# Gated linear attention with a soft mixture of experts: scores by halves with a lasting zero quarter, F32R parts of the log magnitudes, hats in one product, more warming products

## The chip, the cores and the metric

The kernel runs on one core of a Trainium2 chip. The metric is the device time of one execution in microseconds. The core has five engines that matter here, each working through its own list of instructions in order: TensorE (PE in the profile; its weight loads are PEld), VectorE (DVE), ScalarE (ACT), GpSimd (POOL) and SyncE (SP), which here issues the DMA transfers. They wait for each other by semaphores. [...]

## The reference, cut to what matters

Attention has 4 batches, 8 heads, 768 tokens and 48 channels a head. A complex state of 48 x 48 per head decays per channel by a complex gate and takes in the outer product of k and v:

```
mag = sqrt(a_re**2 + a_im**2); scale = minimum(mag, 0.999) / (mag + 1e-6)
for t in range(S):
    S_re, S_im = ar*S_re - ai*S_im + kv[t], ar*S_im + ai*S_re     # a scaled
    y[t] = q[t] @ S_re
```

The outputs, 3072 tokens of 384 channels, go through a soft mixture of 8 experts with 4 slots each: logits = x @ phi; a softmax over all tokens makes 32 slot inputs, each expert is relu(s @ w1) @ w2 with 1024 hidden units, and a softmax over the slots mixes the expert outputs back for every token.

## The kernel before, in words

The recurrence is turned into matrix products over blocks of 128 tokens; a block g is one of 24 (4 batches of 6), three blocks make a unit u, 8 units in all. Tokens of a block lie on the 128 partitions, in an order that `_order` gives: it differs for even and odd blocks (parity), so that the first and last token of a block come to lie where neighbours need them.

For each unit, `gates` (ScalarE and VectorE by turns, L636-658) turns the gates' real parts into log magnitudes and the imaginary parts into tangents, in place in the tile `aat`; `arctan` makes the angles. Then for each block:

- `phase` (L667-691): a triangle of ones (`tri_u`) times the angles sums them over the block (`up`, L676), VectorE removes whole turns (`n` by adding and taking off a magic number, L679; `f = up - n`, L681), and ScalarE takes sine and cosine into `cs`. For blocks that continue a batch, one row takes over the last phase (L673).
- `expo` (L698-711): a triangle (`tri_l`) times the log magnitudes (`lp`, L702, an F32 product of 384 columns), two exponentials into `ee`, and a small transfer of the last row to DRAM (`rows`) for the state's decay.
- `mults` (L719-737): `ee` times q and k (L723; L728 for the first block), then the two hats (`hat0` of q, `hat1` of k), each `ee` times `cs`, on VectorE (L732, two instructions of 768 elements).
- `xpose` (L741-747): transposes of hats on TensorE (`tp`, L744), copied to `hT` by ScalarE.
- `score` (L749-756): four heads at a time, keys times queries, four products of 128 weight columns by 128 columns (`sp`, L752), then one VectorE product with the causal mask `C_MK` over 128 x 512 (`scT`, L756), two buffers.
- `attend` (L764-782): values times scores (L777), state times queries (L779), into `yb`, two heads by turns at PSUM rows 0 and 64, 48 rows each; copied by ScalarE.
- `delta` (L784-797): keys times values (`db`, L790), added to the state `st` and decayed.
- `xform` (L799): output back to tokens-by-channels (`xp`, L802).

The mixture's logits (`lg`, L109), shares and slot sums (`sip`, L173) run per unit between the blocks. At the end come merging, the experts' hidden products (`hp`, L229), the second layer (`op`, L259), and the outputs (`o`, L288, L298; products of F32R operands), with stores by SyncE. The weights of the experts are loaded in 23 chunks (`wload`, L622) into buffers as they come free: 7 `wx` buffers, then those of gates and q/k, then room of closed pools.

The order of all this is written out by hand in the string `ORDER`. Each name (`x17` is the 17th transpose task, `g3` the gates of group 3) stands once for each step of a task; `run` takes the steps in this order and pins every engine's instructions to it. So the string sets what each engine does next; `g` groups, weight loads (`w`), loads of units (`la`, `lq`, `lv`), the first loads (`i`), activation tables (`L`, `T`) and warming products (`wu`) are placed there too. A warming product (`warm`, L901) is an F32 product of 512 columns whose result is not used; before there are four, of the constants.

Of the kernel before, what the change touches and what calls it, by code (L numbers as in the profile page):

```python
# [86 lines left out]
class _Moe:  # L87
# [223 lines left out]
    i0 L0 g0 g0 g0 i6 i1 wu2 wu1 g0 g0 g0 g0 i3 g0 g0 i4 i2 g1 g1 e0 i8 g1 g1 la0 i7 e0 e0 wu0 lv0 T0 t0 g1 t1 e0 p0 p0 p0 p0 p0  # L311
    L1 m0 m0 m0 p1 g1 g1 x0 x0 i5 x2 p1 g1 g1 m0 m0 x2 p1 p2 g2 g2 g2 g2 lq0 e1 e1 e1 x3 x3 e2 e2 e1 e2 x1 x1 p2 g2 g2 D0 e2 D0
    p2 T1 p1 p1 p1 m1 p2 p2 p2 c0 t2 c0 a0 L2 g2 c1 m1 g2 x6 x6 m1 x7 p3 x5 x5 x7 p3 m2 c1 x4 a0 g2 e3 c3 m2 x8 x10 m2 x4 c2 la1
    g3 g3 g3 p3 c3 e3 e3 x11 d0 e5 e5 p4 D0 e5 g3 x10 a0 x8 D1 e4 e4 c2 D1 e3 g3 D1 p4 p4 e4 f0 D1 g3 g3 x9 a1 f0 a1 x9 c4 x11
    wu3 c5 g3 T2 p3 p3 p3 e4 a1 m4 p5 p5 m3 c4 la2 c5 D2 D2 a2 t3 m3 x14 x14 p4 m3 p5 p4 p4 p6 g3 p5 p5 x12 x12 a2 a2 p5 e5 g4
    D2 D3 D3 m4 m4 x16 x16 x15 x15 p6 D2 p6 x18 m5 p7 x13 x13 l0 p7 L3 x18 m5 m5 l0 p7 D3 g4 g4 f1 f1 x17 p8 x17 c6 e7 e7 e7 f2
    g4 c6 c7 f2 e6 e6 e6 x23 x23 x19 g4 g4 lq1 p8 e8 a3 c7 a3 l0 s0 e8 p8 g4 d1 q0 q0 e8 x20 w0 x19 x20 g4 D3 a3 T3 p6 p6 p8 c8
    c8 p8 g4 x21 x21 c9 c9 D4 D4 D4 x22 e6 x22 m6 p7 p7 a4 a4 D4 c10 c11 lv1 m6 x26 t4 p7 p9 m6 p9 c10 p8 p9 a4 x25 x24 s0 D5 D5
    e7 m7 e8 L4 a5 c11 a5 x25 x24 c12 x26 p10 m7 la3 g5 x28 m7 q0 s0 q0 p10 f3 c12 x27 a5 g5 d2 D5 a6 q0 g5 x28 D6 f3 p10 q0 g5
    x30 x30 x27 m8 g5 m8 x29 e9 e9 m8 e9 x31 x31 e10 e10 e9 l1 l1 e10 g5 c13 c13 x29 x34 x34 e11 c14 e11 lq2 e11 g5 p11 g5 c14  # L320
    q1 f4 f4 q1 q1 T4 D6 D6 x33 x35 x35 x32 x32 g5 p11 a6 a6 p11 p11 p9 p9 p9 c15 c15 s0 s0 s0 x33 p11 e10 m10 a7 a7 p10 c17 m9
    p10 t5 c16 a7 p11 D6 lv2 D7 D7 m9 x36 p10 q1 q1 p12 c16 la4 a8 c17 a8 g6 L5 e11 g6 g6 x38 x38 q1 e13 m9 p12 a8 x39 x39 lv3
    e12 D7 D8 D8 x36 e12 e12 x37 m10 x42 p13 m10 x37 g6 w1 l1 s1 x40 c18 x40 g6 x42 c19 D7 g6 x43 x41 e13 e13 d3 c18 a9 c19 a9
    a9 x41 m11 D8 D9 x43 m11 m11 e12 e14 e14 e14 g6 g6 f7 p13 p13 p14 x47 x47 lq3 m12 f7 T5 c21 c21 p12 c20 D9 p12 c20 p12 x45
    t6 x46 x46 x45 s1 p14 D8 f5 f5 x44 p14 x44 a10 a10 s1 l2 la5 p15 p15 m12 x50 D9 x50 e13 m12 p13 p13 p13 c22 e14 g6 x49 x48
    x49 x48 p14 p14 c22 p14 D10 D10 a10 l2 q2 c23 p15 D9 d4 p15 p16 p16 g7 p15 p15 q2 c23 x51 x51 m13 m13 f6 s1 f6 a11 a11 a11
# [756 lines left out]
```

## Time and profile before

| | |
|---|---|
| median of 3 runs | 300.86 us (299.57 to 302.11) |
| the profiled execution | 302.44 us, span 300.6 us |
| busy time TensorE, VectorE, ScalarE | 271.5, 236.5, 213.5 us |
| mean granted clock of TensorE | 0.960 |
| DMA | 54.85 MB, of it 49.61 MB read from HBM |

The span runs from the first to the last instruction. Busy time is the union of an engine's instructions; two that overlap count once. A matmul of F32 leaves two records in the profile, one of F32R leaves one; their ends are modelled, so distances from start to start are more telling than lengths. In a group's row stand line, engine, operation, tiles, shapes and count, then the busy time and the mean length of one in ns, and last the idle time ahead with what ended it. The granted clock is the share of full speed that TensorE's throttle let through.

### The profile page before, as it was taken

The page shows a single profiled execution, that of the slowest core. Times are in us where ns is not written, and L with a number is a line of the kernel's source. Part 1 is how long each engine was busy: PE and PEld are TensorE (multiplying, and loading weights), DVE is VectorE, ACT ScalarE, POOL GpSimd, SP SyncE. Part 2 cuts the span into 40 slices and gives each one's busy share as a digit, 9 for nine tenths or more (in the row PEclk, how much of TensorE's full clock was granted, in tenths as well). Part 3 has the DMA queues.
Part 4 walks back from the last instruction along what each step waited for, and adds up shares of the span by engine and source line. Part 5 has one row for each costly group of instructions (what it writes and reads, how often), then busy time and mean ns, then how long its engine had stood idle before and what let it go on. Part 6 is the DMA issues. An engine that isn't in the chain of part 4 may idle for free.

```text
span 300.6 us, 6641 instructions
## 1 busy us (share of the span) xinstructions
PE 271.5 (90%) x2694; PEld 214.2 (71%) x2694; DVE 236.5 (79%) x453; ACT 213.5 (71%) x377; POOL 2.8 (1%) x7
## 2 busy tenths in 40 slices
PE   0649599989999999899999999999999999999990
PEld 0135488778888877888878887888898997336760
DVE  1468789899999999999998999998979565714350
ACT  4878979789997997896998797996737444402240
POOL 0000000000000000000000000000000002100000
PEclk9966779989999999999999999999999999999997
DMA  6980720391730493735027990456816496589495
GB/s 244 422 219 3 75 86 3 98 313 48 142 98 2 80 295 89 186 126 160 3 15 302 354 375 11 14 190 240 218 19 266 148 423 256 241 342 423 184 384 200
DMA packets 20788, 54.85 MB, mean 182 GB/s; under 512 B 11536, under 2 KB 13456, under 8 KB 16144
## 3 DMA queue, kind: packets, MB, share of 16 engines
q1 hardware_dynamic: 20752, 54.37, 55.2%
q8 instruction: 23, 0.38, 0.6%
q14 instruction: 13, 0.11, 0.1%
HBM read 49.61 MB, written 4.76 MB: 181 GB/s over the span
## 4 chain that ended last, share of the span: by engine, by line
PE 65%; DMA 12%; ACT 11%; DVE 7%; issue 2%; SPq 0%; DVEq 0%; ACTq 0%
PE sp L752 12%; PE tp L744 11%; DMA aat<-in_aa_dram 8%; PE yb L777 6%; PE db L790 5%; DMA rows<-ee 5%; PE lp L702 4%; PE yb L779 4%; PE up L676 4%; PE hp L229 3%; PE op L259 3%; PE xp L802 3%; PE lg L109 2%; PE ep L277 2%; ACT gt L642 2%
## 5 line engine op out<-in xcount | busy, mean ns | idle before, releaser
L747 ACT COPY hT<-tp 96x512 f32<-96x512 f32 x96 | 53.5, 583 | 17.9 <-PE tp L744 17.8
L744 PE MATMUL tp<-cst,hat 128*96 128x128 f32 x384 | 57.2, 287 | 4.0 <-DVE hat L732 3.8
L744 PEld LDWEIGHTS tp<-cst,hat 128*96 128x96 f32 x384 | 45.0, 134 | 13.5 <-issue 5.8
L752 PE MATMUL sp<-hT,hT 96*128 96x128 f32 x384 | 51.6, 282 | 0.9 <-ACT hT L747 0.9
L752 PEld LDWEIGHTS sp<-hT,hT 96*128 96x128 f32 x384 | 47.2, 194 | 5.3 <-issue 2.5
L732 DVE TENSOR_TENSOR hat<-ee,cs 128x768 f32<-128x768 f32 x48 | 44.6, 951 | 2.3 <-PE tp L744 0.9
L777 PE MATMUL yb<-scT,vt 128*48 128x128 f32 x384 | 37.2, 280 | 3.5 <-DVE scT L756 3.5
L756 DVE TENSOR_TENSOR scT<-sp,cst 128x512 f32<-128x512 f32 x48 | 32.6, 684 | 3.7 <-PE sp L752 3.5
L790 PEld LDWEIGHTS db<-vt,hat 128*96 128x96 f32 x320 | 30.2, 165 | 4.2 <-issue 1.7
L790 PE MATMUL db<-vt,hat 128*96 128x48 f32 x320 | 30.8, 246 | 1.3 <-DVE st L795 1.3
L779 PE MATMUL yb<-hT,st 96*48 96x128 f32 x320 | 31.2, 272 | 0.0
L777 PEld LDWEIGHTS yb<-scT,vt 128*48 128x48 f32 x384 | 21.2, 123 | 11.2 <-issue 3.9
L723 DVE TENSOR_TENSOR ee<-ee,qkt 128x768 f32<-128x768 f32 x23 | 21.8, 951 | 4.8 <-DMA rows<-ee 3.3
L676 PE MATMUL up<-aat,cst 128*128 128x384 f32 x48 | 21.5, 532 | 3.2 <-ACT aat L665 2.9
L702 PE MATMUL lp<-aat,cst 128*128 128x384 f32 x48 | 21.5, 531 | 0.9 <-DVE aat L658 0.5
L779 PEld LDWEIGHTS yb<-hT,st 96*48 96x48 f32 x320 | 19.2, 123 | 0.0
L782 ACT COPY yT<-yb 128x512 f32<-128x512 f32 x24 | 14.0, 582 | 6.5 <-PE yb L779 6.5
L648 DVE TENSOR_TENSOR aat<-aat,gt 128x1152 f32<-128x1152 f32 (+2 forms) x9 | 11.0, 1219 | 8.8 <-ACT gt L646 8.8
L805 ACT COPY xs<-xp 128x384 f32<-128x384 f32 x24 | 11.3, 476 | 8.6 <-PE xp L802 8.6
L679 DVE TENSOR_SCALAR n<-up 128x384 f32<-128x384 f32 x24 | 13.2, 550 | 2.6 <-PE up L676 2.5
L802 PE MATMUL xp<-cst,yT 128*128 128x128 f32 x96 | 14.4, 274 | 0.4 <-DVE scT L756 0.4
L706 ACT ACTIVATE ee<-lp 128x384 f32<-128x384 f32 x24 | 11.8, 492 | 4.2 <-PE lp L702 4.0
(134 smaller groups left out, 418.6 us busy)
## 6 DMA issues: line engine op xcount, KB each, us to landing
aat<-in_aa_dram SPq DMA_DIRECT2D x7, 1152.0 KB
qkt<-in_qk_dram SPq DMA_DIRECT2D x7, 1152.0 KB
wx<-in_w_dram SPq DMA_DIRECT2D x7, 1024.0 KB
wx<-in_w_dram SPq DMA_DIRECT2D x5, 1152.0 KB
vt<-in_vv_dram SPq DMA_DIRECT2D x8, 576.0 KB
out_dram<-os SPq DMA_DIRECT2D x8, 384.0 KB
we<-in_w_dram SPq DMA_DIRECT2D x2, 1152.0 KB
wt<-in_w_dram SPq DMA_DIRECT2D x2, 1152.0 KB
```

The source lines that it names most:

```text
L676: PE.matmul(out=up, lhsT=tri_u[par], rhs=ph, start=True, stop=True)
L702: PE.matmul(out=lp, lhsT=tri_l[par], rhs=aat[u][:, 0, j], start=True, stop=True)
L723: DVE.tensor_tensor(out=e, in0=e, in1=qkt[u][:, j], op=ALU.mult)
L732: DVE.tensor_tensor(out=x, in0=e[:, w].rearrange("p (h d) -> p h d", d=D).unsqueeze(2).broadcast_to([P, H, 2, D]), in1=cs[g], op=ALU.mult,)
L744: PE.transpose(out=tp[:, a, :], in_=hat[g][w][:, 4 * hh + a].rearrange("p c d -> p (c d)"), identity=ident)
L747: ACT.copy(out=hT[g, hh, w], in_=tp)
L752: PE.matmul(out=sp[:, a, :], lhsT=hT[g, hh, 1][:, a, :], rhs=hT[g, hh, 0][:, a, :], start=True, stop=True)
L756: DVE.tensor_tensor(out=t, in0=sp, in1=mask[g % 2].unsqueeze(1).broadcast_to([P, 4, P]), op=ALU.mult)
L777: PE.matmul(out=o, lhsT=vt[u][:, j, h, :], rhs=scT[g, hh][:, a, :], start=True, stop=first)
L779: PE.matmul(out=o, lhsT=st[g - 1][:, h, :], rhs=hT[g, hh, 0][:, a, :], start=False, stop=True)
L790: PE.matmul(out=db[:, h, :], lhsT=hat[g][1][:, h].rearrange("p c d -> p (c d)"), rhs=vt[u][:, j, h, :], start=True, stop=True)
L802: PE.transpose(out=xp[:, c].rearrange("p a d -> p (a d)"), in_=yT[g][:, c, :], identity=ident)
```

## The change

- **Scores by halves.** In a block's order the two halves of 64 partitions are early and late tokens (odd blocks have them swapped). A score of four heads becomes eight products: for each head, the early keys (64 weight columns) with all 128 queries, and the late keys with the late 64 queries. Late keys with early queries, all masked to zero, are not computed: that quarter of each of four lasting tiles (`masked`) is set to zero once by GpSimd. Odd heads have the rows of the halves swapped, so that a pair of heads writes the two halves of PSUM's rows; for them the values are loaded a second time with swapped halves (`vs`, `vst`). VectorE's one mask product becomes three: late queries for all rows (256 elements), and early queries for the 64 early rows of even and of odd heads (128 elements each, 64 partitions).
- **F32R parts.** The log magnitudes are split into an F32R part `hi` (a copy by ScalarE) and the rest `lo` (a subtraction by VectorE), as two more steps of `gates`; `lp` becomes two F32R products that add up. The triangle is copied to an F32R tile once (`tr0`).
- **Phase.** The magic number is added by ScalarE (`n`), VectorE takes it off and subtracts `up` in one instruction; the sign of `f` turns and the sines' scales with it.
- **Hats in one product.** One VectorE instruction of 1536 elements per block for both hats, two buffers of the pair.
- **Warming.** Fourteen warming products in place of four, of a zero tile `blank`, so that they need no transfer; they stand in `ORDER` among the first steps, the last two further behind.
- **Buffers and loads.** 6 `wx` buffers in place of 7; the last weight chunk is loaded into a room of its own at the pools' swap; output tiles take other buffers; the scratch memory for dynamic DMA is set to 1024. The first loads come in another order: all gates of unit 0, the constants, phi, v, the masks, the gates of unit 1, and only then q and k.
- **ORDER** is another string throughout.

The core of the diff:

```diff
+HB = P // 2
+FIRST = (0, HB)
+LAST = (HB, 0)
 def _order(parity):
-    o = list(range(P))
-    for p, t in SWAPS[parity]:
-        o[p] = t
+    o = [(p + HB * parity) % P for p in range(P)]
+    a, b = LAST[parity], LAST[parity] + HB - 1
+    o[a], o[b] = o[b], o[a]
...
 def gates(x):
...
         DVE.scalar_tensor_tensor(out=ar, in0=ar, scalar=W_MAX, in1=t, op0=ALU.min, op1=ALU.subtract)
+        yield "g9"
+        hi, lo = (w[:, j0:j1] for w in parts[u])
+        ACT.activation(out=hi, in_=ar, func=AF.Copy)
+        yield "g10"
+        DVE.tensor_tensor(out=lo, in0=ar, in1=hi.bitcast(F32), op=ALU.subtract)
...
 def phase(u, j):
...
-        DVE.tensor_scalar(out=n, in0=up, scalar1=MAGIC, scalar2=MAGIC, op0=ALU.add, op1=ALU.subtract)
+        ACT.activation(out=n, in_=up, func=AF.Identity, bias=kb[:, 4:5])
+        yield "p2b"
-        DVE.tensor_tensor(out=f, in0=up, in1=n, op=ALU.subtract)
+        DVE.scalar_tensor_tensor(out=f, in0=n, scalar=MAGIC, in1=up, op0=ALU.subtract, op1=ALU.subtract)
...
 def expo(u, j):
...
-        PE.matmul(out=lp, lhsT=tri_l[par], rhs=aat[u][:, 0, j], start=True, stop=True)
+        for x in range(2):
+            PE.matmul(out=lp, lhsT=tri_r[par], rhs=parts[u][x][:, j], start=x == 0, stop=x == 1)
...
 def mults(g):
...
+        DVE.tensor_tensor(out=e, in0=e, in1=qkt[u][:, j], op=ALU.mult)
+        yield "m0"
+        x = wk.tile([P, 2, H, 2, D], F32, name="hat", bufs=BUF["hat"])
+        DVE.tensor_tensor(
+            out=x,
+            in0=e.rearrange("p w (h d) -> p w h d", d=D).unsqueeze(3).broadcast_to(sh),
+            in1=cs[g].unsqueeze(1).broadcast_to(sh),
+            op=ALU.mult,
+        )
...
 def score(g, hh):
+        lo = HB * par
+        early, late_ = slice(lo, lo + HB), slice(HB - lo, P - lo)
-        for a in range(4):
-            PE.matmul(out=sp[:, a, :], lhsT=hT[g, hh, 1][:, a, :], rhs=hT[g, hh, 0][:, a, :], start=True, stop=True)
+        for c in range(2):
+            for rows_, cols in ((early, slice(0, P)), (late_, late_)):
+                for b in range(2):
+                    a = 2 * c + b
+                    o = (rows_.start + HB * b) % P
+                    PE.matmul(out=sp[o : o + HB, a, cols], lhsT=hT[g, hh, 1][:, a, rows_], rhs=hT[g, hh, 0][:, a, cols], start=True, stop=True)
         yield "c1"
-        DVE.tensor_tensor(out=t, in0=sp, in1=mask[g % 2].unsqueeze(1).broadcast_to([P, 4, P]), op=ALU.mult)
+        t = masked[par][hh % BUF["scT"]]
+        DVE.tensor_tensor(
+            out=t[:, :, :, late_], in0=sv[:, :, :, late_], in1=mask[par][:, :, late_].unsqueeze(1).broadcast_to([P, 2, 2, HB]), op=ALU.mult
+        )
+        for b in range(2):
+            o = (lo + HB * b) % P
+            r = slice(o, o + HB)
+            DVE.tensor_tensor(
+                out=t[r, :, b, early], in0=sv[r, :, b, early], in1=mask[par][r, b, early].unsqueeze(1).broadcast_to([HB, 2, HB]), op=ALU.mult
+            )
...
 def attend(g):
...
-                            PE.matmul(out=o, lhsT=vt[u][:, j, h, :], rhs=scT[g, hh][:, a, :], start=True, stop=first)
+                            w = vst[u][:, j, h // 2, :] if b else vt[u][:, j, h, :]
+                            PE.matmul(out=o, lhsT=w, rhs=scT[g, hh][:, a, :], start=True, stop=first)
...
 def warm(x):
-        PE.matmul(out=wp, lhsT=ident, rhs=cst[:, 0:512], start=True, stop=True)
+        PE.matmul(out=wp.rearrange("p (a c) -> p a c", a=4), lhsT=blank, rhs=blank.unsqueeze(1).broadcast_to([P, 4, P]), start=True, stop=True)
...
-    for x in range(4):
+    for x in range(14):
         at("wu", warm, x)
```

More of the change, by code (lines that the diff above doesn't have):

```diff
@@ L310 @@
 ORDER = """
[L311 to L326, printed above, removed]
@@ new lines @@
+    p6 a2 e4 m4 c5 p6 la2 p5 p5 x15 f1 g3 e5 x12 f1 x12 p6 D2 a2 g3 D3 a2 D3 m5 g4 x14 x14 L3 x13 x13 p7 p7 p7 w0 wu9 m4 g4 c7
+    g3 m5 l0 l0 x18 x18 p7 g4 c7 q0 q0 f0 f0 f2 f2 l0 s0 e6 e6 x19 x19 e6 g4 c6 e7 e7 lv1 x17 x17 g4 g4 d1 e7 p8 x16 x16 c9 e8
+    e8 e8 c6 D2 e6 e7 g4 q0 g4 D3 T3 m6 p8 a3 p8 t4 c9 c8 x22 x21 x20 la3 c8 x23 x22 q0 a3 a3 p6 e8 p8 d2 D4 D4 p6 p6 D3 a4 x21
+    a4 p8 g4 s0 p8 p8 p9 x20 c10 p9 lq2 p7 p7 p7 m6 x23 c11 D4 D5 c10 x25 g4 x26 m7 p9 D4 L4 p9 s0 s0 p10 a4 q0 x27 m7 g5 g5 q0
@@ L561, in _polar @@
     tri_u = [cst[:, C_TU : C_TU + P], cst[:, C_TU + P : C_TL]]
-    tri_l = [cst[:, C_TL : C_TL + P], cst[:, C_TL + P : C_MK]]
-    mask = [cst[:, C_MK : C_MK + P], cst[:, C_MK + P : C_SEL]]
+    tri_t = cp.tile([P, 2 * P], F32R, name="tri_t")
+    tri_r = [tri_t[:, 0:P], tri_t[:, P : 2 * P]]
+    mask = [cst[:, C_MK + 2 * P * x : C_MK + 2 * P * (x + 1)].rearrange("p (b t) -> p b t", b=2) for x in range(2)]
     ones = cst[:, C_ONE:C_END]
-    kb = cp.tile([P, 4], F32, name="kb")
+    kb = cp.tile([P, 5], F32, name="kb")
     DVE.memset(kb[:, 0:1], 1.0)
@@ L582, in _polar @@
     moe = _Moe(nc, cp, ys, ps2, cst, phi_sb)
-    aat, qkt, vt = {}, {}, {}
+    aat, qkt, vt, vst = {}, {}, {}, {}
     def load_a(u):
@@ L596, in load_v @@
         SP.dma_start(out=vt[u], in_=vv[u])
+        vst[u] = io.tile([P, UB, 4, D], F32, name="vst")
+        SP.dma_start(out=vst[u], in_=vs[u])
     def load_first(x):
-        if x == 0:
+        if x in (0, 3, 4) and 0 not in aat:
             aat[0] = io.tile([P, 2, UB, HD], F32, name="aat")
-        if x == 2:
+        if x in (2, 7) and 0 not in qkt:
             qkt[0] = io.tile([P, UB, 2, HD], F32, name="qkt")
@@ L658, in gates @@
         DVE.scalar_tensor_tensor(out=ar, in0=ar, scalar=W_MAX, in1=t, op0=ALU.min, op1=ALU.subtract)
+        yield "g9"
+        if u not in parts:
+            parts[u] = [eo.tile([P, UB, HD], F32R, name=f"w{x}", bufs=1) for x in range(2)]
+        hi, lo = (w[:, j0:j1] for w in parts[u])
+        ACT.activation(out=hi, in_=ar, func=AF.Copy)
+        yield "g10"
+        DVE.tensor_tensor(out=lo, in0=ar, in1=hi.bitcast(F32), op=ALU.subtract)
     cs, fr = {}, {}
@@ L910, in _polar @@
         at("i", load_first, x)
+    at("tr", lambda: DVE.tensor_copy(out=tri_t, in_=cst[:, C_TL:C_MK]) and None)
     def w1_chunk(y):
@@ L917, in w2_chunk @@
         return wsl[NW1 + n][:, cols]
[L919 to L920 removed]
+    for x in [(wx, rx)] * BUF["wx"] + [(io, ra)]:
+        at("w", lambda x=x: wload(x[0], **x[1]))
     def hidden():
@@ L941, in os_tile @@
         if n not in late["os"]:
-            late["os"][n] = io.tile([P, W2C], F32, name="os", tag=("qkt", "aat")[n % 2])
+            pl, kw = ((io, rq), (io, ra), (io, rq), (wx, rx))[n]
+            late["os"][n] = pl.tile([P, W2C], F32, name="os", tag=kw["name"])
         o = 2 * UB * HA * x
```

144 lines of the change are left out of this document (73 added, 71 removed).

## The prediction

> **What bounds the kernel now.** I read the page's first part, then a table of stages, then the groups by line, then short pieces of the timeline.
>
> ```profile
> PE 271.5 (90%) x2694; PEld 214.2 (71%) x2694; DVE 236.5 (79%) x453; ACT 213.5 (71%) x377; POOL 2.8 (1%) x7
> ...
>
> ```
>
> TensorE is busy 271.5 of 300.6 us, but this is an average over three different stages. The table of stages (length, busy time of PE, PEld, DVE, ACT, POOL, granted clock, DMA share, GB/s) parts them:
>
> ```profile
> 0.00:45.00 45.00, 27.39 (x119) 17.69 (x120) 28.49 (x47) 34.36 (x49) 0.20 (x4) 0.81 0.58 175
> 45.00:60.00 15.00, 14.64 (x133) 11.90 (x133) 13.77 (x21) 12.97 (x21) 0.00 (x0) 1.00 0.18 50
> 60.00:200.00 140.00, 136.73 (x1389) 116.27 (x1388) 133.67 (x239) 122.68 (x214) 0.00 (x0) 0.99 0.50 142
> 200.00:250.00 50.00, 49.98 (x562) 43.86 (x563) 38.78 (x82) 28.49 (x62) 0.32 (x1) 1.00 0.61 224
> 250.00:301.00 51.00, 42.71 (x500) 24.49 (x494) 21.79 (x67) 15.02 (x34) 2.27 (x3) 0.96 0.75 296
> ...
> 36.00:45.00 9.00, 9.00 (x53) 7.61 (x53) 8.02 (x11) 6.93 (x9) 0.00 (x0) 0.71 0.28 102
> ```
>
> Up to 45 us no engine is full: the start hangs on a chain from engine to engine. From 45 to 250 us TensorE is busy 14.64 + 136.73 + 49.98 = 201.4 of 205 us, so it sets the end there. But from 60 to 200 us VectorE stands at 133.67 of 140 (95%) and ScalarE at 122.68 (88%): what TensorE gains, VectorE takes back soon. From 200 to 250 us VectorE (78%) and ScalarE (57%) have room, and TensorE alone binds. The tail after 250 us (experts, outputs) is barely touched.
>
> **The change part by part.** The groups of the lines concerned, and the nearest ones for what is new:
>
> ```profile
> L752 PE MATMUL sp<-hT,hT 96*128 96x128 f32 x384 | 51.6, 282 | 0.9 <-ACT hT L747 0.9
> ...
> L732 DVE TENSOR_TENSOR hat<-ee,cs 128x768 f32<-128x768 f32 x48 | 44.6, 951 | 2.3 <-PE tp L744 0.9 <-PE db L790 0.9
> ...
> L756 DVE TENSOR_TENSOR scT<-sp,cst 128x512 f32<-128x512 f32 x48 | 32.6, 684 | 3.7 <-PE sp L752 3.5
> ...
> L702 PE MATMUL lp<-aat,cst 128*128 128x384 f32 x48 | 21.5, 531 | 0.9 <-DVE aat L658 0.5 <-DVE f L681 0.3
> ...
> L679 DVE TENSOR_SCALAR n<-up 128x384 f32<-128x384 f32 x24 | 13.2, 550 | 2.6 <-PE up L676 2.5
> ...
> L706 ACT ACTIVATE ee<-lp 128x384 f32<-128x384 f32 x24 | 11.8, 492 | 4.2 <-PE lp L702 4.0
> ...
> L658 DVE SCALAR_TENSOR_TENSOR aat<-aat,gt 128x1152 f32<-128x1152 f32 x7 | 9.4, 1349 | 0.0
> ...
> L665 ACT ACTIVATE aat<-aat 128x1152 f32<-128x1152 f32 x7 | 8.1, 1157 | 0.0
> ...
> L178 DVE SCALAR_TENSOR_TENSOR acc<-acc,al,sip 96x384 f32<-96x384 f32 x7 | 4.2, 606 | 2.4 <-PE sip L173 2.2
> ...
> L113 DVE COPY ls<-lg 96x128 f32<-96x128 f32 x8 | 2.2, 281 | 0.4 <-PE lg L109 0.3
> ...
> L252 DVE COPY hz<-htp 128x256 f32<-128x256 f32 x4 | 1.6, 418 | 8.3 <-PE htp L245 8.3
> ...
> L658 DVE SCALAR_TENSOR_TENSOR aat<-aat,gt 128x768 f32<-128x768 f32 x1 | 1.0, 959 | 1.0 <-ACT gt L656 1.0
> ...
> L658 DVE SCALAR_TENSOR_TENSOR aat<-aat,gt 128x384 f32<-128x384 f32 x1 | 0.6, 559 | 0.7 <-ACT gt L656 0.7
> ```
>
> Matmuls overlap, so their price is the step from start to start, and for that I use the timeline (start, length, engine, line):
>
> ```profile
> 58.39 0.39 PE L777 MATMUL yb<-scT,vt 128*48 128x128 f32 x4
> 58.61 0.39 PE L779 MATMUL yb<-hT,st 96*48 96x128 f32 x4
> 58.93 0.64 PE L744 MATMUL tp<-cst,hat 128*96 128x128 f32 x4
> 59.41 0.81 PE L676 MATMUL up<-aat,cst 128*128 128x384 f32 x2
> 60.06 0.60 PE L744 MATMUL tp<-cst,hat 128*96 128x128 f32 x4
> 60.59 0.42 PE L777 MATMUL yb<-scT,vt 128*48 128x128 f32 x4
> ...
> 126.17 0.17 PEld L777 LDWEIGHTS yb<-scT,vt 128*48 128x48 f32 x4 [0.18 <-DVE scT L756]
> ...
> 148.88 1.95 PE L752 MATMUL sp<-hT,hT 96*128 96x128 f32 x16
> 150.67 0.49 PE L744 MATMUL tp<-cst,hat 128*96 128x128 f32 x3
> ...
> 290.31 3.27 PE L298 MATMUL o<-sr,er 128*128 128x256 f32 x24
> ```
>
> *Scores.* Now: 16 records (two scores of four heads; an F32 product leaves two records) take 150.67 - 148.88 = 1.79 us, so 0.895 us a score, 0.11 us a record. The products of L777/L779 write 48 rows each at row 0 and row 64 of PSUM by turns: four records (two heads) start 0.22 us after the four before (58.39, 58.61), half of 4 x 0.11. Two heads run side by side on the two column halves of the array. The new score does the same: per two heads four records of 128 columns (0.22 us) and four of 64 columns (0.11 us), 0.33, so 0.66 us a score. 48 x 0.235 = -11.3 us. The halves follow each other as 0, 64, 64, 0, an order that no row shows; if they pair anyway, that is the price (else a rival, below).
>
> *Changes of layout on the array.* From L779 to the full-width tp: 58.93 - 58.61 = 0.32 where the step would be 0.22: 0.10 us lost. From tp back to L777: 60.59 - 60.06 = 0.53 against 4 x 0.11 = 0.44: 0.09 lost. Counted in the two orders written out by hand, products of different width meet 86 times before and 136 times after, since the scores join the narrow ones: 50 x 0.093 = +4.7 us.
>
> *The sum over log magnitudes in two F32R parts.* Now a product of 384 columns steps 0.65 us (60.06 - 59.41, the like product of L676). F32R products leave one record: 24 of 256 columns in 3.27 us with their waits, 0.13 each. So 384 columns lie between a quarter of F32 (0.16) and 1.5 x 0.13 = 0.20. Two of them 0.33 to 0.40; I take 0.36, between the ends, since the 0.13 holds waits for evictions: 24 x 0.29 = -7.0 us. The parts cost ScalarE a copy per group like L665 (8.1 + 0.8 + 0.5, from 1157 ns by elements: +9.4 us) and VectorE a subtraction like L658 (9.4 + 1.0 + 0.6: +11.0 us).
>
> *Phase.* The rounding moves from VectorE (L679, -13.2 us) to ScalarE (like L706, +11.8 us). The remaining VectorE step is of L178's kind (606 ns against the old subtraction's, about L679's 550): +1.3 us.
>
> *Hat.* One product of 1536 elements: 768 elements take 951 ns and 384 (the row at 18.05 us, below) 560, so 951 + 768 x (951 - 560) / 384 = 1733 ns against 2 x 951: 24 x 0.17 = -4.1 us. Its first transposes wait 0.8 us longer for it, hidden where other heads' products queue on TensorE, exposed in the first block.
>
> *Masks.* One instruction of 512 elements (684 ns) becomes one of 256 (418, L252) and two of 128 (281, L113): 980 ns, 48 x 0.296 = +14.2 us. The lasting zero quarter is written once by GpSimd, which idles. The copy of the triangle to F32R is +0.4 us.
>
> VectorE in all: -13.2 + 1.3 - 4.1 + 14.2 + 11.0 + 0.4 = +9.6 us by durations. But instructions overlap their neighbours:
>
> ```profile
> 151.19 1.29 DVE L756 TENSOR_TENSOR scT<-sp,cst 128x512 f32<-128x512 f32 x2
> ...
> 40.38 1.07 ACT L747 COPY hT<-tp 96x512 f32<-96x512 f32 x2 [1.12 <-PE tp L744]
> ```
>
> Two masks take 1.29, not 1.37: 0.08 a piece. With 58 instructions more (96 masks, 9 subtractions, 1 copy, less 24 roundings and 24 hats), 4.6 us of it vanish: +5.0 us. Bounds: +9.6 without overlap, 0 if the 128-element pieces overlap more. ScalarE: +21.2 us, less 33 x 0.10 (1.07 against 2 x 0.583) = +18 us.
>
> *Warming products, loads, buffers.* Ten more products of 512 columns, 4/3 of 0.65 = 0.87 us each at full clock. Twelve stand where TensorE waits for the first blocks' chain, two (the last) inside the full stage; before, one of four did: +0.9 us. What they may bring: from 36 to 45 us TensorE is full at a clock of 0.71, so up to 9 x 0.29 = 2.6 us. The second copy of v adds 288 KB to each of eight units, 2.36 MB, at the tail's 296 GB/s 8 us of DMA time, covered by a DMA share of 0.50 in the long stage; uncovered only in the tail, one weight chunk (1 MB, 3.4 us) comes later, since one buffer fewer takes weights early. The new order loads unit 1's gates ahead of the first q and k: hidden behind the gates' chain, at most 1.18 MB at that rate, 4 us, if it is not. SyncE issues the eight copies one by one ahead of the small transfers of the decay rows, for which VectorE's next product waits; those are due a block later. I cost all this at nothing, with up to +4.
>
> *Start.* The first sum now waits for copy and subtraction of 384 elements (0.5 + 0.56 = 1.1 us), the first transpose for both hats:
>
> ```profile
> 18.05 0.56 DVE L728 TENSOR_TENSOR ee<-ee,qkt 128x384 f32<-128x384 f32 x1 [0.50 <-DMA rows<-ee]
> 18.71 0.96 DVE L732 TENSOR_TENSOR hat<-ee,cs 128x768 f32<-128x768 f32 x1
> ```
>
> 0.95 + 1.73 instead of 0.56 + 0.96, +1.2. So +2.3 against -2.6 from the clock: 0, bounds -2.6 to +2.3.
>
> **The sum.** How much of it lies in 45 to 250 us, the stage table of single lines tells (first L752's PE and PEld, then L702's):
>
> ```profile
> 0.00:45.00 45.00, 4.32 (x25) 3.98 (x26) 0.81 0.58 175
> ...
> 200.00:250.00 50.00, 12.56 (x100) 11.66 (x98) 1.00 0.61 224
> ...
> 0.00:45.00 45.00, 5.03 (x8) 1.62 (x8) 0.81 0.58 175
> ...
> 200.00:250.00 50.00, 2.43 (x6) 0.91 (x6) 1.00 0.61 224
> ```
>
> Only 25 of 384 score records and 8 of 48 lp records lie before 45 us, so some 0.94 and 0.83 of both terms count. TensorE: 201.4 - 10.6 + 4.4 - 5.8 + 0.9 = 190.3 us. VectorE: 186.2 + 0.85 x 5.0 = 190.5. ScalarE: 164.1 + 0.85 x 18 = 179.4. Two engines are now level. TensorE's 11.1 us saved are split: from 200 us on (100 score records, 6 lp) 12.5 x 0.235 - 12.9 x 0.093 - 3 x 0.29 with its sign, 2.6 us, pass whole, since the others have room. Of the other 8.5 us I let half through (4.2): VectorE at 95% leaves 6 us of 140, the wider buffers (two hats, four score tiles) let some of its work slide behind 200 us. Start 0, tail 0: -6.8 us. The profiled execution, 302.44 us (span 300.6 and 1.8 around it), would be 295.6; it lies 1.6 above the median of the runs, 300.86, so **294.1 us**.
>
> **The rivals.**
> *All of it comes through* (0.20). VectorE's pieces overlap more and its work moves behind 200 us; the start gains the clock's 2.6: -11.1 - 2.6 = -13.7, 287.2 us. For it: ScalarE and VectorE have 21 and 11 us of idle in 200 to 250 us. Against: gates of later units must be done before.
> *VectorE and ScalarE take over* (0.16). Nothing passes before 200 us, the start costs 2.3: -2.6 + 2.3, 300.6 us. For it: of the 0.85 x 18 and 0.85 x 5.0 us, 140 of 205 parts fall in 60 to 200 us, so ScalarE would stand at (122.68 + 10.4) / 140 = 95% there, VectorE at 98%.
> *Weight loads come one by one* (0.04). A score has 16 loads of 64 columns. What a load costs where the products are short shows in the chain of waits (start, length):
>
> ```profile
> 89.05 1.32 PE db L790 x16
> ```
>
> These loads have 96 columns for 48 streamed, 0.083 us a step; 64 columns so take 0.055, 0.88 us a score: nothing saved on scores, TensorE -2.3 us in all, half of it -1: 299.8 us. Against it stands the row at 126.17: four loads within 0.17 us, each 0.12 long. [...]
> *The halves do not pair* (0.14), the slower side. In the order 0, 64, 64, 0 each half of the array gets two products in a row. If TensorE keeps their order strictly, only the neighbours of different halves overlap, by one record of each: per two heads the eight records take 4 x 0.11 + 4 x 0.055 = 0.66 us one after another, less some 0.18 of overlap, 0.48, so 0.96 us a score: +3.1 instead of -11.3. With layout changes (+4.7), lp (-7.0) and warming (+0.9) TensorE has 1.7 us more to do; with VectorE and ScalarE nearly full and the start at +2.3, 304.9 us. With no pairing at all (1.32 us a score) +20 us. It decides from 0.93 us a score on, where 48 x 0.035 equals what lp leaves.
>
> **How the numbers follow.** The forecast has 0.46; its own spread is 291 to 298. A measurement of this kernel tells about 1% (3 us) from no change. Faster by over 1% (under 297.9): 0.44 of the forecast and 0.20, 0.64. Within: 0.02, 0.16 and 0.04, less a few that fall outside, 0.21. Slower: 0.15. The range runs from the first rival, 286, to the last one, 305.
>
> **What would show it.** A score of 0.62 to 0.70 us from start to start, lp 0.33 to 0.40 us, TensorE's busy time between 45 and 245 us near 190 and VectorE's nearly equal, VectorE's sum at 240 to 247 us, ScalarE's at 230 to 235. The forecast is wrong if scores take over 0.9 us, if the clock before 45 us stays near 0.8 and the first block's attention comes over 3 us later, or if the tail shows TensorE waiting for weights.

## The result, and the profile after

The changed kernel takes 303.06 us in the median of 13 runs, the kernel before 301.03 us in 13 runs beside them. The ratio is 1.0068, with a 95% interval of 1.0045 to 1.0090: slower by two thirds of a per cent, where 2.2% faster was forecast (294.1 against 300.86 us). The ratios, and the times of a kernel without a ratio, leave out single runs that lie over 1.5% above the fastest of that kernel. The profiled execution is the shortest of its 13 (300.97 us, span 299.1), that of before (302.44 us) was one of the longer ones, so their spans say nothing about which kernel is faster; the shape of the work does.

The page's first part and the clock, after:

```profile
PE 272.1 (91%) x3098; PEld 207.0 (69%) x3098; DVE 246.2 (82%) x511; ACT 231.5 (77%) x410; POOL 4.8 (2%) x12
...
PEclk9778899999999999999999999999999999999996
```

The same stages as before:

```profile
0.00:45.00 45.00, 32.73 (x142) 17.68 (x142) 28.27 (x48) 36.91 (x55) 2.25 (x9) 0.85 0.53 172
45.00:60.00 15.00, 14.00 (x155) 11.29 (x153) 14.73 (x25) 14.55 (x25) 0.00 (x0) 1.00 0.69 193
60.00:200.00 140.00, 134.21 (x1647) 111.33 (x1646) 137.21 (x269) 132.61 (x234) 0.00 (x0) 1.00 0.51 157
200.00:250.00 50.00, 49.57 (x692) 43.33 (x690) 44.67 (x106) 33.11 (x68) 1.45 (x1) 1.00 0.51 164
250.00:301.00 51.00, 41.56 (x474) 23.36 (x470) 21.30 (x66) 14.34 (x32) 1.14 (x3) 0.94 0.81 324
```

Between 60 and 200 us VectorE (third of the busy times) is now the fullest engine: 137.21 of 140 us, 98%, where it had 133.67; TensorE went from 136.73 down to 134.21, ScalarE from 122.68 up to 132.61. Over 45 to 250 us VectorE has 196.6 us (+10.4), TensorE 197.8 (-3.6), ScalarE 180.3 (+16.1). TensorE did get less work there, and the time is not shorter: VectorE has taken its place as the fullest engine.

The groups of the changed lines:

```profile
L740 DVE TENSOR_TENSOR hat<-ee,cs 128x1536 f32<-128x1536 f32 x24 | 42.0, 1751 | 1.2 <-ACT cs L703 0.7
...
L785 DVE TENSOR_TENSOR scT<-sp,cst 64x128 f32<-64x128 f32 x96 | 27.5, 286 | 1.3
...
L779 DVE TENSOR_TENSOR scT<-sp,cst 128x256 f32<-128x256 f32 x48 | 19.9, 415 | 0.9 <-PE sp L774 0.5
L939 PE MATMUL wp<-blank 128*128 128x512 f32 x28 | 19.5, 808 | 2.8 <-POOL blank L934 2.8
L715 PE MATMUL lp<-w,tri_t 128*128 128x384 f32 x48 | 15.6, 403 | 2.4 <-ACT w L667 1.8 <-DVE w L669 0.3 <-ACT ee L721 0.2
...
L690 ACT ACTIVATE n<-up,kb 128x384 f32<-128x384 f32 x24 | 13.9, 580 | 3.0 <-PE up L687 2.5 <-ACT cs L703 0.3
...
L669 DVE TENSOR_TENSOR w<-aat,w 128x1152 fp32r<-128x1152 f32 x7 | 9.4, 1346 | 0.0
```

The masks cost VectorE 19.9 + 27.5 = 47.4 us (before 32.6), the hats 42.0 (44.6). The timeline shows more than the sums. A score on TensorE, and the three mask pieces of one score on VectorE (start, length, engine, line):

```profile
106.83 0.89 PE L774 MATMUL sp<-hT,hT 96*64 96x128 f32 x16
107.65 0.85 PE L174 MATMUL sip<-xs,d 128*32 128x384 f32 x6
```

```profile
148.89 0.41 DVE L779 TENSOR_TENSOR scT<-sp,cst 128x256 f32<-128x256 f32 x1
149.31 0.61 DVE L785 TENSOR_TENSOR scT<-sp,cst 64x128 f32<-64x128 f32 x2
149.84 0.60 DVE L179 SCALAR_TENSOR_TENSOR acc<-acc,al,sip 96x384 f32<-96x384 f32 x1
```

The score takes 107.65 - 106.83 = 0.82 us with the change of layout at its end. So the halves do pair, in the order 0, 64, 64, 0 too. The masks take 149.84 - 148.89 = 0.95 us a score, where one mask took 0.60. The first piece does not overlap the second (0.42 from start to start for 0.41 of length), and the two pieces of 64 rows take 0.61, more than twice 0.286, so they do not overlap each other. The start partitions differ: one of the two starts at partition 0, the other at 64. This is an odd block, where the piece at 64 comes first; in even blocks it comes last, and then the first two pieces overlap (0.33 us from start to start for 0.41 of length, from 153.45 us on) and the last one overlaps neither neighbour (0.29 us behind a piece of 0.27, 0.33 to the next instruction for its own 0.29), again 0.95 us in all. It is not a wait for a semaphore: of the 96 small pieces all but one wait for none of VectorE's own.

### The profile page after: what moved, and what is told of

Same layout as the page of the kernel before. It is cut to its first block, busy times and chain, and to the rows that moved or that the text cites. A ratio compares the mean times of both kernels' runs of the same rounds, so it can differ in the third digit from the quotient of the medians.

```text
span 299.1 us, 7564 instructions
## 1 busy us (share of the span) xinstructions
PE 272.1 (91%) x3098; PEld 207.0 (69%) x3098; DVE 246.2 (82%) x511; ACT 231.5 (77%) x410; POOL 4.8 (2%) x12
## 4 chain that ended last, share of the span: by engine, by line
PE 43%; DVE 41%; ACT 6%; issue 4%; DMA 4%; SPq 0%; DVEq 0%; ACTq 0%
DVE hat L740 7%; PE tp L752 6%; PE sp L774 4%; DVE scT L785 4%; PE yb L809 4%; DVE ee L735 4%; PE op L260 4%; PE hp L230 4%; PE yb L811 4%; DVE scT L779 3%; PE db L822 3%; DVE f L693 3%; PE up L687 3%; DMA rows<-ee 2%; DVE aat L662 2%
## 5 line engine op out<-in xcount | busy, mean ns | idle before, releaser
L752 PE MATMUL tp<-cst,hat 128*96 128x128 f32 x384 | 54.8, 280 | 3.3 <-DVE hat L740 2.6
L752 PEld LDWEIGHTS tp<-cst,hat 128*96 128x96 f32 x384 | 42.7, 130 | 12.9 <-issue 8.0
L740 DVE TENSOR_TENSOR hat<-ee,cs 128x1536 f32<-128x1536 f32 x24 | 42.0, 1751 | 1.2 <-ACT cs L703 0.7
L774 PEld LDWEIGHTS sp<-hT,hT 96*64 96x64 f32 x768 | 35.9, 137 | 10.0 <-issue 3.7
L774 PE MATMUL sp<-hT,hT 96*64 96x128 f32 (+1 forms) x768 | 40.3, 251 | 1.0 <-DVE scT L785 0.7
L809 PE MATMUL yb<-scT,vst 128*48 128x128 f32 x192 | 36.0, 277 | 0.0
L785 DVE TENSOR_TENSOR scT<-sp,cst 64x128 f32<-64x128 f32 x96 | 27.5, 286 | 1.3
L939 PE MATMUL wp<-blank 128*128 128x512 f32 x28 | 19.5, 808 | 2.8 <-POOL blank L934 2.8
L779 DVE TENSOR_TENSOR scT<-sp,cst 128x256 f32<-128x256 f32 x48 | 19.9, 415 | 0.9 <-PE sp L774 0.5
L809 PEld LDWEIGHTS yb<-scT,vst 128*48 128x48 f32 x192 | 20.0, 122 | 0.4 <-DVE scT L785 0.3
L715 PE MATMUL lp<-w,tri_t 128*128 128x384 f32 x48 | 15.6, 403 | 2.4 <-ACT w L667 1.8
```

The source lines that it names most:

```text
L740: DVE.tensor_tensor(out=x, in0=e.rearrange("p w (h d) -> p w h d", d=D).unsqueeze(3).broadcast_to(sh), in1=cs[g].unsqueeze(1).broadcast_to ...
L752: PE.transpose(out=tp[:, a, :], in_=hat[g][w][:, 4 * hh + a].rearrange("p c d -> p (c d)"), identity=ident)
L774: PE.matmul(out=sp[o : o + HB, a, cols], lhsT=hT[g, hh, 1][:, a, rows_], rhs=hT[g, hh, 0][:, a, cols], start=True, stop=True)
L779: DVE.tensor_tensor(out=t[:, :, :, late_], in0=sv[:, :, :, late_], in1=mask[par][:, :, late_].unsqueeze(1).broadcast_to([P, 2, 2, HB]), op ...
L785: DVE.tensor_tensor(out=t[r, :, b, early], in0=sv[r, :, b, early], in1=mask[par][r, b, early].unsqueeze(1).broadcast_to([HB, 2, HB]), op=A ...
L809: PE.matmul(out=o, lhsT=w, rhs=scT[g, hh][:, a, :], start=True, stop=first)
```

## The experiments

The ratio of each is to the kernel before, run beside it on the same chip; the changed kernel stands at 1.0068 [1.0045, 1.0090] on this scale, and 0.01 is 3.0 us. My theory after the result was that VectorE had become the bound until 200 us, and its rivals that TensorE still was, or ScalarE.

**no_early_masks.** The two `DVE.tensor_tensor` of the loop over `b` in `score` are taken out.

```diff
-        for b in range(2):
-            ...
-            DVE.tensor_tensor(out=t[r, :, b, early], in0=sv[r, :, b, early], in1=..., op=ALU.mult)
```

> The changed kernel with the two 128-element mask products of each score left out, so the early-by-early quarter of the scores stays zero. 96 VectorE instructions of 286 ns go, some 19 us from start to start; TensorE's work stays. If VectorE sets the pace between 45 and 250 us, the time falls by 10 to 17 us against the changed kernel (303), to 286 to 293. If TensorE sets it, by no more than 2 us, 301 to 303. If ScalarE does, likewise under 3 us.

Measured: 0.9804 [0.9733, 0.9875], 8.0 us less than the changed kernel. VectorE counts, but of the 96 instructions of 0.28 us (27 us) less than a third came through, and under the 10 us expected: the next engine stands close behind.

```profile
60.00:200.00 140.00, 136.51 (x1707) 114.93 (x1705) 126.09 (x216) 137.22 (x240) 0.00 (x0) 1.00 0.53 162
```

With VectorE at 126 of 140 us, TensorE (136.5) and ScalarE (137.2) are full.

**no_split.** `lp` from one F32 product again, the steps for `hi` and `lo` taken out.

```diff
-        for x in range(2):
-            PE.matmul(out=lp, lhsT=tri_r[par], rhs=parts[u][x][:, j], start=x == 0, stop=x == 1)
+        PE.matmul(out=lp, lhsT=tri_l[par], rhs=aat[u][:, 0, j], start=True, stop=True)
```

> The changed kernel with the F32R split undone: one F32 product for the log magnitudes, no copy by ScalarE (-9.5 us), no subtraction by VectorE (-11 us), TensorE +24 x 0.2 = +5 us. VectorE or ScalarE as the bound: 5 to 9 us less than the changed kernel, 294 to 298. TensorE as the bound: 4 to 5 us more, 307 to 308.

Measured: 0.9927 [0.9885, 0.9968], 4.3 us less than the changed kernel, somewhat short of the 5 to 9 expected, and faster than the kernel before. More work for TensorE, with less for the other two, makes it faster: TensorE alone is not the bound.

**full_score.** Four whole products and one mask.

```diff
+        for a in range(4):
+            PE.matmul(out=sp[:, a, :], lhsT=hT[g, hh, 1][:, a, :], rhs=hT[g, hh, 0][:, a, :], start=True, stop=True)
...
+        DVE.tensor_tensor(out=scT[g, hh], in0=sp, in1=mask[g % 2][:, 0].unsqueeze(1).broadcast_to([P, 4, P]), op=ALU.mult)
```

> The changed kernel with the scores by halves undone: four products of 128 weight columns, one mask product of 512 elements, no second copy of the values. VectorE loses 96 instructions, some 7 us from start to start; TensorE gains 48 x 0.235 - 4.7 = 6.6 us of work. VectorE as the bound: 3 to 7 us less, 296 to 300. TensorE as the bound: 6 us more, 309.

Measured: 0.9945 [0.9921, 0.9970], 3.7 us less. Again the part that serves TensorE costs more on VectorE than it brings.

**pe_more.** Each transpose `xp` of L834 issued twice (`for _ in range(2):` around it).

> The changed kernel with every transpose of the attention's output done twice: TensorE +24 x 0.44 = +10.6 us, nothing else. If TensorE still sets the pace: 9 to 11 us more, 312 to 314. If VectorE does before 200 us and TensorE only after: the seven blocks after 200 us count, 2 to 4 us more, 305 to 307.

Measured: 1.0175 [1.0129, 1.0221], 3.2 us more for 10.6 us of TensorE work: about the share of the seven blocks after 200 us, as expected if TensorE binds only there.

**act_more.** ScalarE's copy `xs` of L837 issued twice.

> The changed kernel with ScalarE's copy of the transposed output (128x384, L837) done twice: ScalarE +24 x 0.37 = +9 us from start to start. By the doubled transposes (+10.6 us of TensorE cost 4.0) and the left-out masks (-19 us of VectorE gave 7.8) both have a share near 0.4. If the three engines share the pace, ScalarE has a share of 0.15 to 0.4: 1.5 to 3.5 us more than the changed kernel. If only VectorE and TensorE count: under 1 us more.

Measured: 1.0147 [1.0057, 1.0237], 2.4 us more, with an interval of 2.7 us to each side. Whether ScalarE has a share is not settled.

**few_warm.** Ten of the fourteen names `wu` taken out of `ORDER`.

> The changed kernel with four warming products in place of fourteen: two ahead of everything, one ahead of the first phases, one after the first blocks' transposes. If warming pays by its clock, 1 to 3 us more than the changed kernel and a granted clock under 0.85 before 45 us. If the ten products are a load on TensorE (8.7 us at full clock, most of it in idle time): 1 to 3 us less.

Measured: 1.0085 [1.0049, 1.0122], the changed kernel's time within the intervals, though the granted clock fell as expected:

```profile
0.00:45.00 45.00, 25.95 (x88) 14.68 (x88) 25.91 (x42) 33.65 (x50) 2.25 (x9) 0.65 0.51 157
```

The clock before 45 us is 0.65 in place of 0.85, and the time moves by 0.5 us, less than the intervals. Neither expectation (1 to 3 us either way) held. That the clock at the start is worth nothing does not follow: leaving ten products out also takes their load off TensorE, and the two may cancel. Nor does one profile tell the clock of a kernel: among those that keep all fourteen products the same stage shows 0.73 (masks_p0) to 0.96 (no_split).

**dve_round.** The rounding of the phase back on VectorE.

```diff
-        ACT.activation(out=n, in_=up, func=AF.Identity, bias=kb[:, 4:5])
         yield "p2b"
+        DVE.tensor_scalar(out=n, in0=up, scalar1=MAGIC, scalar2=None, op0=ALU.add)
```

> The changed kernel with the rounding of the phase put back on VectorE (+24 x 0.55 = +13 us there, ScalarE -12 us). With shares of 0.4 for VectorE and 0.15 to 0.4 for ScalarE: 1 to 4 us more. If VectorE alone is the bound: 8 to 13 us more. If ScalarE is: 5 us less or better.

Measured: 1.0495 [1.0387, 1.0604], 12.9 us more for 13.2 us more of VectorE's busy time (259.4 against 246.2), while ScalarE's fell by 8.2 (223.3). What is added to VectorE comes through whole, within an interval of about 3 us. This is the theory's clearest mark; the shares of 0.4 that I had read out of the first four runs hold only for taking work away, where the next engine stops the gain.

**old_scores_no_split.** The edits of no_split and full_score together.

> The changed kernel with the F32R split and the scores by halves both undone; hats in one product, rounding on ScalarE, warming and order stay. TensorE +11.6 us of work, VectorE -18, ScalarE -9.5. The two undone alone gave -4.1 and -3.2. If VectorE is the bound until 200 us and TensorE has room: -5 to -8, 296 to 299 on the scale of the kernel before at 302.4, faster than both kernels. If TensorE is then the bound: -1 to -3, about like one of them alone.

Measured: 1.0030 [0.9987, 1.0073], 1.1 us less than the changed kernel. Undone together they bring less than either alone:

```profile
60.00:200.00 140.00, 139.11 (x1406) 117.15 (x1405) 123.36 (x204) 129.39 (x230) 0.00 (x0) 1.00 0.50 149
```

TensorE is at 139.1 of 140 us: now it is the bound. The three kernels show the seesaw, VectorE full in the changed one, TensorE full here, the best ones between.

**masks_p0.** Both small mask pieces start at partition 0.

```diff
-            r = slice(o, o + HB)
+            r = slice(0, HB)
+            part = late_ if o else early
-                out=t[r, :, b, early], in0=sv[r, :, b, early], in1=mask[par][r, b, early]...
+                out=t[r, :, b, part], in0=sv[r, :, b, part], in1=mask[par][r, b, part]...
```

> The changed kernel with both 128-element mask products of a score on partitions 0 to 63: the one of partitions 64 to 127 is replaced by a second pass over late queries on partitions 0 to 63, so one early quarter in two stays zero. Size and count are the same. In the trace of the changed kernel the piece that starts at partition 64 takes 295 ns against 273 and steps 0.29 to 0.33 us to and from its neighbours, without overlap, so a score's three pieces take 0.94 us. If the start partition is the reason, they take 0.73 us, VectorE loses 10 us, and the time falls by 3 to 5 us against the changed kernel. If the small size is the reason: no change.

Measured: 0.9799 [0.9741, 0.9857], 8.1 us less, more than expected and as much as without the pieces altogether. As many instructions of the same size; their timeline:

```profile
152.22 0.41 DVE L779 TENSOR_TENSOR scT<-sp,cst 128x256 f32<-128x256 f32 x1
152.56 0.47 DVE L786 TENSOR_TENSOR scT<-sp,cst 64x128 f32<-64x128 f32 x2
152.95 0.41 DVE L779 TENSOR_TENSOR scT<-sp,cst 128x256 f32<-128x256 f32 x1
```

A score's masks take 152.95 - 152.22 = 0.73 us. (In odd blocks 0.85: there the second pass writes what the first piece has just written, and the trace shows it waiting for VectorE's own semaphore. 0.79 on average.) In these rows each piece overlaps the next one by 0.07 to 0.08 us, as the two masks of before did at one start partition (1.29 us for two of 0.684). 48 x (0.95 - 0.79) = 7.7 us of VectorE, and the time fell by 8.1. The stage from 60 to 200 us:

```profile
60.00:200.00 140.00, 137.43 (x1699) 114.63 (x1697) 137.54 (x276) 137.06 (x242) 0.00 (x0) 1.00 0.53 163
```

TensorE, VectorE and ScalarE are at 137 of 140 us each: the balance that the forecast had counted on.

**masks_p64.** Its mirror, both pieces at partitions 64 to 127: `r = slice(HB, P)`, `part = early if o else late_`.

> The mirror of masks_p0: both 128-element mask products of a score on partitions 64 to 127; the one of partitions 0 to 63 is replaced by a second pass over late queries on partitions 64 to 127, so the other early quarter in two stays zero. If every instruction that starts at partition 64 runs without overlap: the three pieces take about 0.33 + 3 x 0.31, no less than 1.0 us, VectorE +3 to +5 us, the time like the changed kernel or up to 5 us more. If only the change from one start partition to another costs: like the changed kernel or a little less. If fewer filled quarters by themselves made masks_p0 fast: 8 us less, as there.

Measured: 1.0126 [1.0087, 1.0164], 1.8 us more than the changed kernel. It leaves out as much as masks_p0, so what masks_p0 leaves out is not why it is fast.

```profile
141.02 0.41 DVE L779 TENSOR_TENSOR scT<-sp,cst 128x256 f32<-128x256 f32 x1
141.46 0.50 DVE L786 TENSOR_TENSOR scT<-sp,cst 64x128 f32<-64x128 f32 x2
141.99 0.26 DVE L165 COPY d<-mt 128x96 f32<-128x96 f32 x1
```

The two pieces overlap each other here (0.50 for two), but neither the instruction ahead (0.44 from start to start) nor the one behind (0.53 for 0.50): 0.97 us. An odd block's score, in which the first small piece writes nothing that the piece ahead has written, has the same steps: 153.56, 154.00, 154.53 us. So it is the change from one start partition to the other that costs the overlap, each way; in the changed kernel there are two of them a score.

**only_halves.** The kernel before, in its own order, with nothing but the scores by halves (row order, `vs`, masks in three pieces).

> The kernel before with the scores by halves alone (row order, second copy of the values, masks in three pieces), its own order and all else as before. TensorE 48 x 0.235 - 50 x 0.093 = -6.6 us, VectorE 48 x 0.34 = +16 us. If VectorE is as near to being the bound as TensorE (95% until 200 us): 3 to 8 us more than the kernel before. If TensorE alone is: 4 to 6 us less.

Measured: 1.0397 [1.0326, 1.0468], 12.0 us more, beyond the 3 to 8 expected. **only_halves_p0** is the same with the edit of masks_p0:

> The kernel before with the scores by halves alone, the mask pieces of partitions 64 to 127 replaced by a second pass over late queries on partitions 0 to 63 as in masks_p0 (one early quarter in two stays zero). only_halves took 12 us more than the kernel before. If the start partition is the reason there too: VectorE -10 us against only_halves, 6 to 10 us less, 304 to 308. If TensorE's part of the halves is: as only_halves, 314.

Measured: 1.0128 [1.0051, 1.0206]: 8.1 us of the 12 are gone. The cause holds in the old order too, which also shows that the halves alone are a clear loss; the other parts of the change and its new order win most of it back. The 3.9 us left are of the size of the masks' remaining 48 x (0.79 - 0.60) = 9 us, less the 6.6 us that the expectation gave TensorE; this was not tested further.

**pool_lo.** `POOL.tensor_tensor` in place of `DVE.tensor_tensor` for `lo`.

> The changed kernel with the subtraction of the F32R split on GpSimd, which idles: VectorE -11 us, TensorE and ScalarE as they are. VectorE as the bound until 200 us: 3 to 6 us less than the changed kernel, about as much as undoing the split (4.1) or more, since TensorE keeps its saving. Rival: GpSimd is slow or disturbs VectorE at SBUF, and the first sums come later: 0 or more.

Measured: 1.0230 [1.0147, 1.0313], 4.9 us more: the rival.

```profile
L684 DVE SCALAR_TENSOR_TENSOR aat<-f,aat 1x384 f32<-1x384 f32 x20 | 16.9, 846 | 0.3
...
L669 POOL TENSOR_TENSOR w<-aat,w 128x1152 fp32r<-128x1152 f32 x7 | 21.7, 3094 | 165.4 <-ACT w L667 165.4
```

GpSimd takes 3094 ns for what VectorE does in 1346, and VectorE's one-row correction (L684) grows from 545 to 846 ns on average. Three of the 20 took 2.3 to 2.9 us, the others about 545 ns. The trace shows what held the three:

```profile
67.34 2.63 POOL L669 TENSOR_TENSOR w<-aat,w 128x1152 fp32r<-128x1152 f32 x1 [17.90 <-ACT w L667]
67.44 2.95 DVE L684 SCALAR_TENSOR_TENSOR aat<-f,aat 1x384 f32<-1x384 f32 x1
```

Each starts while GpSimd subtracts and ends 0.41 us after it (here 70.38 against 69.97). A product of `ee` with q and k is held likewise (2.35 us in place of 0.95, from 148.70 us on). All of these read two tiles in SBUF; instructions that read a PSUM tile at such a time keep their lengths (a mask product at 124.30 us takes 0.40, and the mean lengths of L779, L785 and L693 stay at 415, 286 and 545 ns). Where VectorE's instructions kept theirs although they read SBUF alone, GpSimd's subtraction took 3.1 to 4.0 us instead of 2.6. So VectorE's busy time fell by 1.8 us (246.2 to 244.4), not by 11. How much of the 4.9 us comes from this, and how much from sums that start later, was not separated. **pool_lo_row** puts that correction on GpSimd as well (a scaling and an addition on `POOL`).

> As pool_lo, and the one-row correction of the phases (20 instructions of 545 ns, L684) as two instructions on GpSimd too: VectorE -20 us in all. VectorE as the bound: 5 to 8 us less than the changed kernel, then TensorE and ScalarE bind. Rival: the row stands on the chain from block to block, and a slower GpSimd makes TensorE wait for it: no better than pool_lo, or worse.

Measured: 1.0454 [1.0370, 1.0538], 11.7 us more. From 60 to 200 us VectorE is busy for only 119.6 of 140 us and TensorE for 126.4, so no engine is full. This fits the rival, that the row stands on the chain from block to block and GpSimd's time counts there; GpSimd holding up VectorE, as in pool_lo, is in it too.

**lasting_psum, one_mask, one_mask_no_split.** One lasting PSUM tile for the scores, so that a single mask over everything may read it; three tiles in turn for the rest.

```diff
-NTR = 4
+NTR = 3
-        sp = ps2.tile([P, 4, P], F32, name="sp", tag="tr", bufs=NTR)
+        sp = spt
```

> Control for the next kernel: the changed kernel with the scores in one lasting PSUM tile, set to zero once, and three PSUM tiles in turn for the rest in place of four; masks in three pieces as before. Fewer tiles in turn can only cost: 0 to 4 us more than the changed kernel.

> As the control, and one mask product of 512 elements over all rows and queries: the quarter that is not computed holds old finite numbers or zeros, and the mask is zero there. Nothing is left out. VectorE per score 0.60 in place of 0.94 us, -16 us; TensorE keeps its halves. If the pieces that start at partition 64 are what ate the gain: 6 to 10 us less than the control, near or under 297, faster than both kernels. If the halves on TensorE cost by themselves (layout changes, waits): under 3 us less.

> As one_mask, with the F32R split undone as in no_split: VectorE -11, ScalarE -9.5, TensorE +5 us. If VectorE and ScalarE still bind after one_mask: 2 to 4 us less than one_mask. If TensorE binds by then: 2 to 5 us more.

Measured: 1.1497 [1.1402, 1.1593] (347.65 us) for the control, 328.1 and 329.5 us for one_mask beside 301.41 of the kernel before, 1.0853 [1.0758, 1.0947] (327.6 to 330.9 us) for one_mask_no_split. The control was to cost 0 to 4 us and cost 43 more than the changed kernel. All three also compute other values than the reference, for a cause that stays open, against what the expectation of one_mask says; I read their times only against each other.

```profile
PE spt L777 <- DVE scT L788: 23.2, 15, 2.2
DVE scT L782 <- PE spt L777: 22.0, 19, 3.8
```

In the control TensorE and VectorE wait for each other at the one tile, 23 and 22 us. One mask in place of three takes some 19 us off, with 16 us expected of VectorE, but in this lock-step any saving there would show. That one_mask and one_mask_no_split lie level says as little, one engine waiting for the other as it does. Whether the halves with a cheap mask would beat both kernels is not answered.

**hybrid.** Scores by halves for the first four heads of a block, whole products with one mask for the others.

```diff
+        if hh == 0:
+            yield from halved(g, hh)
+            return
```

> The changed kernel with scores by halves for the first four heads of a block only, whole products and one mask for the other four. VectorE -24 x 0.34 = -8 us, TensorE +3.3 us. full_score (all eight heads) gave -3.2 us against the changed kernel, with TensorE then full. If the two engines trade places between: -3 to -6 us, 298.5 to 301.5 where the kernel before has 302.4. If TensorE and VectorE only hand the pace to each other: -1 to -3.

Measured: 0.9976 [0.9947, 1.0006], 2.8 us less than the changed kernel, inside the second expectation (the two engines only hand the pace to each other) and not clearly faster than the kernel before. The fastest kernel with the whole computation remains no_split, at 0.9927.

## Why the prediction was wrong, point by point

- **The pairs of the scores: right.** 0.82 us with a change of layout at the end; two scores in a row take 1.49 us (from 146.70 to 148.19), so a score that is followed by another takes 0.67, against the forecast's 0.66. The rivals "the halves do not pair" and "weight loads come one by one" fell: 16 loads fit into these 0.67 us, which 0.88 us of loads alone would not have allowed; the 32 loads of the two scores take 1.42 us in all, from 146.70 us on.
- **The log magnitudes: too good.** Four products of two sums:

```profile
153.84 0.94 PE L715 MATMUL lp<-w,tri_t 128*128 128x384 f32 x4
154.62 1.47 PE L752 MATMUL tp<-cst,hat 128*96 128x128 f32 x12
```

  0.78 us for two sums, 0.39 each; a sum by itself took 0.43 to 0.45, since the first F32R product after others steps 0.26 us where the later ones step 0.17 (0.26 + 3 x 0.17 from 153.84 us on). The later ones are close to the quarter of F32's 0.65 us that the prediction took as its lower end (0.16); the first lies outside its 0.16 to 0.20. The term was -7.0 us and is about -5.
- **ScalarE: about right.** +18.0 us (213.5 to 231.5) against +18; the rounding took 580 ns a piece, not 492, other pieces a little less.
- **The masks: the step that failed.** The prediction priced three pieces at 980 ns and took 0.08 us of overlap off each of the additional ones: 6.5 us more for VectorE. The lengths were right (47.4 - 32.6 = 14.8 us more, against 14.2). But the pieces take 0.95 us from start to start against 0.60, so 48 x 0.35 = 16.8 us. The overlap, taken from rows of instructions that all start at partition 0, does not exist where the start partition changes (masks_p0, masks_p64). The trace of before already had this, in a line that the prediction did not look at: the one-row correction of the phase (L673) starts at partition 0 in even blocks and at partition 32 in odd ones. Block 16, then block 17, each with the instruction behind it:

```profile
143.55 0.54 DVE L673 SCALAR_TENSOR_TENSOR aat<-f,aat 1x384 f32<-1x384 f32 x1
144.02 0.34 DVE L689 TENSOR_SCALAR n<-f 128x384 int32<-128x384 int32 x1
...
150.62 0.55 DVE L673 SCALAR_TENSOR_TENSOR aat<-f,aat 1x384 f32<-1x384 f32 x1
151.19 1.29 DVE L756 TENSOR_TENSOR scT<-sp,cst 128x512 f32<-128x512 f32 x2
```

  The even block's correction lets the next one start after 0.47 us of its 0.54, the odd block's only after 0.57; none of the twelve corrections of odd blocks overlaps a neighbour. An estimate from these rows, 0.1 us for each of two changes a score, gives 48 x 0.2 = 9.6 us, near the 10.3 by which the term was too small. VectorE's busy time rose by 9.7 us (236.5 to 246.2), not 5.0, which is the bound without overlap (+9.6) that the prediction had named and not used; that it was not more is luck, since the other terms of this sum came out 5 to 6 us lower than priced. The step is nearly all of the miss: masks_p0, where the overlap is back, stands at 0.9799, and 294.1 us would have been 0.978 (masks_p0 leaves a part of the scores at zero, with as many instructions). From start to start the traces show 0.42 to 0.44 us for the 0.41 us piece where the start partition changes and 0.34 where it doesn't; with the row at 150.62 us in view the prediction would have had to stay near its bound of +9.6 us.
- **Half of TensorE's saving let through: wrong in consequence.** VectorE had 6 us of room in 140 and was to get 3; it got more, was full, and nothing passed before 200 us. From the end of ScalarE's copy of the first attention block to that of the 17th the profiles show 145.5 us before, 148.1 after, and 143.5 in masks_p0. That is the rival "VectorE and ScalarE take over" (300.6 us), to which I had given 0.16, with its shares (VectorE 98%, ScalarE 95%); the measured time lies 2 us above even this one. dve_round shows that at that point VectorE's work counts one for one.
- **Start and warming: about zero, but the two parts are not shown.** In the profiles the first block's copy ends at 48.8 us after the change and at 48.9 before. The clock of 0.85 in place of 0.81 lies within what kernels with the same fourteen products show (0.73 to 0.96), and few_warm does not separate the clock's gain from the products' load. Whether +2.3 and -2.6 us met there, or both are nearer to nothing, stays open.
- **Tail, loads, buffers: right.** No wait of TensorE for weights in the tail: after 250 us none of its waits ends with a transfer.
- **The signs that were named did not catch it.** Scores took under 0.9 us, the first block came no later, the tail did not wait, and VectorE's sum of 246.2 us lies in the 240 to 247 that was to confirm the forecast, though the forecast itself had reckoned with 241.5. A sign has to be as narrow as the room that it guards, here 3 us on VectorE.
- **Two small slips in the sums.** The range's lower end, 286, is named as the first rival's, whose sum is 287.2; and the -2.3 us of "weight loads come one by one" leave out the 0.9 us for warming. Neither moves the forecast.

## What to carry to other kernels

Where two engines are near full, price a change on the second one with the same care as on the first, and let nothing through that the second has no room for: here added work counted whole (12.9 us for 13.2 in dve_round), and saved work only up to the next engine (8.0 us for 27 in no_early_masks). Splitting an instruction into pieces by partition is not free of order: look at the step from start to start where the start partition changes, not at the length of a piece (0.95 us here for three pieces that took 0.73 from one start partition). Before an idle engine is counted as room, ask what its instructions do to the others; GpSimd was idle (4.8 us busy) and still no help (4.9 us more in pool_lo).
